# Two pieces of VectorE work given to other engines in the first pairs of a fused attention and expert kernel

## The chip, the cores and the metric

The kernel runs on one core of one Trainium2 chip. The core has five engines with a queue each, and each queue runs its instructions in order: TensorE (PE, with its weight loads PEld), VectorE (DVE), ScalarE (ACT), GpSimd (POOL) and SyncE (SP, which here only issues transfers). The metric is the device time of one execution in microseconds (us), the median of several runs.

## The reference, cut to what matters

Attention by random features feeds a gated expert layer, and that feeds a second expert layer. There are 8 batches of 576 tokens, 8 heads of 64, a model width of 512 and a hidden width of 1024.

```python
proj = q @ w_phi                                  # also for k, per head
proj = proj - max(abs(proj), axis=-1)
q_p, k_p = concat(exp(proj), exp(-proj))          # 256 features
num = q_p @ (k_p.T @ v);  den = q_p @ sum(k_p) + 1e-6
x = num / den                                     # 8 heads side by side: width 512
xk = mu_k * x + (1 - mu_k) * x_prev               # x_prev: the token before
xr = mu_r * x + (1 - mu_r) * x_prev               # these two are "the mixes"
y = sigmoid(xr @ w_r) * (relu(xk @ w_k) ** 2 @ w_v)
h = relu(y @ w_in);  out = (h * sigmoid(conv3(h)) @ w_out)
```

## The kernel before, in words

The attention works on pairs of heads, 32 of them (4 for each batch), numbered from 0. For each pair, TensorE projects the keys (`pk`, two tiles of 512 columns) two pairs ahead and the queries (`pq`) one pair ahead, and the last 64 tokens apart (`p`). VectorE takes the largest magnitude of each (`mx`) and subtracts it (`t`, `centre`, lines 328 to 332). TensorE turns the queries (`pt`, `pr`), ScalarE takes the exponentials (`kp`, `kr`, `qf`), TensorE sums keys and values (`pkv`, copied to `kvf` by ScalarE) and multiplies (`pn`). `results` (lines 411 to 429) scales: two small additions and a reciprocal give `rd`, two instructions of VectorE scale the first 512 tokens of the two heads into `xn` (tokens by width), and a third scales the last 64 tokens (line 428). TensorE turns `xn` into `xT` by way of `px` and `pr`, and ScalarE copies it (`column`, `column_end`).

When the four pairs of a batch are there, the first expert layer takes the batch in two halves of 288 tokens (`moe(u)`, u from 0 to 15). The mixes of a half are made in `mix(u, j)`, lines 483 to 502, j = 0 for xk and 1 for xr, in four parts of 128 rows. For u = 0, ScalarE writes `mu * x` to `mh` and VectorE adds `(1 - mu) * x_prev` in one instruction (line 491). For later halves a temporary `xf` is made likewise, then split into a coarse part (`mh`, ScalarE) and the rest (`ml`, VectorE). The products are `psk` (w_k), `psr` (w_r) and `psv` (w_v); `kf`, `kh`, `sg` and `x` are what ScalarE and VectorE make of them.

The weights come in 64 bit floats and are converted on the way, in 20 steps, numbered here from 0: steps 0 to 7 are w_k, 8 and 9 half of w_r, 10 to 13 half of w_v, 14 and 15 the rest of w_r, 16 to 19 the rest of w_v. A step (lines 204 to 219) is a load `raw` by SP (512 KB, three buffers), `h<-raw` on ScalarE, `h<-h` on GpSimd, `h<-h` and twice `h<-raw,h` on VectorE, and a transfer by SP into its place (`wkl<-h`, `wrh<-h`, `wvl<-h`). SP's queue takes these transfers in a fixed order: the write of step n stands ahead of the load of step n + 3.

TensorE's order is written out by hand. The orders of the other engines come from the framework's list scheduler, which runs a model of the engines while the program is built: a changed instruction can move its neighbours. `behind` (line 69) pins an instruction behind the last one given to its engine. The temporaries of the expert layers come from a pool of four buffers (`tmps`). `ORDER` (line 24) says in which order the buffers of four tile groups come up in the last stage, where it serves to choose offsets.

Of the kernel before, what the change touches and what calls it, by code (L numbers as in the profile page):

```python
# [8 lines left out]
F32 = mybir.dt.float32  # L9
F32R = mybir.dt.float32r  # L10
U32 = mybir.dt.uint32
AF = mybir.ActivationFunctionType
ALU = mybir.AluOpType
AX = mybir.AxisListType

P = 128
B, H, S, D = 8, 8, 576, 64
# [3 lines left out]
FC = DFF // P  # L21
TMPS = 4
XT = 6
ORDER = {"kh": (0, 3, 2, 1), "kl": (0, 3, 2, 1), "mh": (0, 1), "ml": (0, 1)}
PSM = 3


# [2 lines left out]
MS, SLOW, SR = 4, 8, {4: 6, 5: 6, 6: 7, 7: 9}  # L30
# [5 lines left out]
HS = S // 2  # L36
# [9 lines left out]
def fused_kernel(ctx: ExitStack, tc: tile.TileContext, qk, va, wphi, ones2, mu, wk, wv, wr, win, wout, cw, out):  # L46
# [29 lines left out]
    T, V, A, G = Noted(nc.tensor), Noted(nc.vector), Noted(nc.scalar), Noted(nc.gpsimd)  # L76
# [3 lines left out]
    tmps = ctx.enter_context(tc.tile_pool(name="tmps", bufs=TMPS))  # L80
# [3 lines left out]
    def f(x):  # L84
        return x.bitcast(F32)
# [29 lines left out]
    mu1 = const.tile([P, 2, KC], F32, name="mu1")  # L115
# [13 lines left out]
    def place(tag, name, c, dtype=F32R):  # L129

        return tagged(tag, name, dtype)[:, 7:7 + (KC if tag[0] == "m" else 2) * HS].rearrange("p (a n) -> p a n", a=c)

    def place2(tag, name, i, n):

        o = -(BASE[tag] + 16 * i) % 64
        return tagged(tag, name)[:, o:o + n]
# [53 lines left out]
    with ExitStack() as p1:  # L190
# [66 lines left out]
        for h in range(2):  # L257
            for w in ((wr, wrh, wrl), (wv, wvh, wvl)):
                n = w[1].shape[1] // 2
# [9 lines left out]
        xT = {}  # L269
# [141 lines left out]
        def results(Pi, qf):  # L411

            kv = kvs.pop(Pi)
            pn = [psa.tile([P, 512], F32, tag="at", name="pn")[:, :n * V1].rearrange("p (a n) -> p a n", n=V1) for n in (5, 4)]
            prods = [(0, 0, j, c) for j in range(4) for c in range(2)] + [(0, None, 4, c) for c in range(2)]
            prods += [(1, 1, j, c) for j in range(4) for c in range(2)]
            for b_, h, j, c in prods:
                for r in range(2):
                    h_, o = (r, 512) if h is None else (h, j * P + 64 * r)
                    T.matmul(pn[b_][64 * r:64 * r + 64, j], qf[h_][:, c, o:o + 64], kv[:, c, h_], start=(j == 0 and c == 0), stop=(j == 4 - b_ and c == 1))  # L420
            rd = pool.tile([P, 9], F32, tag="rd4", bufs=2, name="rd")
            V.tensor_scalar(rd[:, :5], pn[0][:, :, D], 1e-6, None, ALU.add)
            V.tensor_scalar(rd[:, 5:], pn[1][:, :, D], 1e-6, None, ALU.add)
            V.reciprocal(rd, rd)
            xn = xns[Pi] = pool.tile([P, 5, P], F32, tag="xn", bufs=1, name="xn")
            for h in range(2):
                V.tensor_tensor(xn[:, :4, D * h:D * h + D], pn[h][:, :4, :D], rd[:, 5 * h:5 * h + 4].unsqueeze(2).to_broadcast([P, 4, D]), ALU.mult)
            V.tensor_scalar(xn[:, 4].rearrange("p (a n) -> p a n", a=2), pn[0][:, 4:5, :D].to_broadcast([P, 2, D]), rd[:, 4:5], None, ALU.mult)
            del ts[Pi]

        xns = {}
# [5 lines left out]
        def block(Pi):  # L437
# [26 lines left out]
            if Pi >= 0:  # L464
                results(Pi, qf)
# [17 lines left out]
        def mix(u, j):  # L483

            b, hf = divmod(u, 2)
            o = hf * HS
            hi = place("mh", f"mh{j}", KC, F32R if u else F32)
            if u == 0:
                for c in range(KC):
                    (A.behind if j else A.do)("activation", hi[:, c], xT[b, c][:, 1 + o:1 + o + HS], AF.Copy, scale=mu0[:, j, c:c + 1])  # L490
                    (V.behind if j else V.do)("scalar_tensor_tensor", hi[:, c], xT[b, c][:, o:o + HS], mu1[:, j, c:c + 1], hi[:, c], ALU.mult, ALU.add)
                return hi, hi
            lo = place("ml", f"ml{j}", KC)
            for c0 in range(0, KC, 2):
                xf = tmps.tile([P, 2, HS], F32, tag="tmp", name="xf")
                for c in range(c0, c0 + 2):
                    late = (u, j) == (1, 1)
                    (A.behind if late else A.do)("activation", xf[:, c - c0], xT[b, c][:, 1 + o:1 + o + HS], AF.Copy, scale=mu0[:, j, c:c + 1])
                    (V.behind if late else V.do)("scalar_tensor_tensor", xf[:, c - c0], xT[b, c][:, o:o + HS], mu1[:, j, c:c + 1], xf[:, c - c0], ALU.mult, ALU.add)
                A.copy(hi[:, c0:c0 + 2], xf)  # L500
                V.tensor_tensor(lo[:, c0:c0 + 2], xf, f(hi[:, c0:c0 + 2]), ALU.subtract)
            return hi, lo
# [3 lines left out]
        def mix_next(u, j):  # L506
            if (u, j) in mixed:
                return True
            if u >= 2 * B or any((u // 2, c) not in xT for c in range(KC)):
                return False  # L510
            mixed[u, j] = mix(u, j)
            if j and u % 2:
                done[0] = u // 2 + 1
            return True
# [145 lines left out]
    with ExitStack() as p2:  # L660
# [17 lines left out]
        def load_x2(i):  # L678
            lo, hi = U * i, U * i + U
            xs_ = []  # L680
            for c in range(0, KC, 2):
                if i % 2:
                    xh, xl = [place2(t, m_, ORDER[t][c // 2], 2 * U).rearrange("p (a n) -> p a n", a=2) for t, m_ in (("mh", "xh"), ("ml", "xl"))]
                else:
# [12 lines left out]
        def up(i, fc, xs_):  # L697
# [34 lines left out]
            if fc >= 4 and end:  # L732
                if not fc % 2:
                    last[:] = [place2(t_, m_, ORDER[t_][fc // 2 - 2], U + 64 + n) for t_, m_ in (("mh", "gh"), ("ml", "gl"))]
                o = fc % 2 * (U + 64)
                gh, gl = [x[:, o:o + n] for x in last]
            elif fc < 4:
                gh, gl = [place2(t_, m_, ORDER[t_][fc], n) for t_, m_ in (("kh", "gh"), ("kl", "gl"))]
            else:
# [101 lines left out]
```

## Time and profile before

| | us |
|---|---|
| median of 3 runs | 1203.96 |
| lowest and highest run | 1203.6, 1205.41 |
| the profiled execution | 1204.29 |
| its span, first to last instruction | 1202.3 |
| PE busy | 1187.5 (99%) |
| DVE busy | 751.4 (62%) |
| ACT busy | 687.7 (57%) |
| POOL busy | 142.9 (12%) |

Times are counted from the first instruction, and 1.99 us of the profiled execution lie outside the span. The granted TensorE clock is 1.00 in every stretch. The shares hide the beginning: in the first 64 us VectorE is nearly always busy and TensorE is not, and after about 123 us TensorE hardly ever stops.

### The profile page before, as it was taken

Reading aid. Unit: us, or ns where it says so; the run is one execution under the profiler, and the core shown is the slowest. Engines: PE = TensorE matmul, PEld = TensorE weight load, DVE = VectorE, ACT = ScalarE, POOL = GpSimd, SP = SyncE. Lnnn points to the kernel's source line nnn. Section 1 sums busy time; section 2 is a strip of 40 time slices with the busy share of each in tenths; the row PEclk is TensorE's granted clock in tenths of the full one; section 3 lists DMA queues with packets and bytes.
Section 4 is the critical chain, followed back from the end, with each engine's and each line's share of the span. In section 5 each row is a group of like instructions: output and inputs, shape, how many; then the busy total and the mean of one; then the engine's idle time right before and its main releaser. Section 6 shows DMA issues by size and latency. Waiting matters only on the chain.

```text
span 1202.3 us, 28950 instructions
## 1 busy us (share of the span) xinstructions
PE 1187.5 (99%) x11842; PEld 1097.7 (91%) x11842; DVE 751.4 (62%) x1525; ACT 687.7 (57%) x1604; POOL 142.9 (12%) x353
## 2 busy tenths in 40 slices
PE   7999999999999999999999999999999999999998
PEld 7887999999999999999999999998888888888888
DVE  7988776576675765767646534426557556645744
ACT  5765865576565664665645534426546555655653
POOL 2122101111111110211000000001101111111200
PEclk9999999999999999999999999999999999999999
DMA  6666222234232322332110004050221121022021
GB/s 231 222 194 230 62 76 59 87 94 125 88 94 77 107 96 87 95 98 88 50 52 23 12 21 161 20 195 1 71 71 29 42 71 40 31 71 59 12 71 36
DMA packets 57252, 100.76 MB, mean 84 GB/s; under 512 B 8864, under 2 KB 38304, under 8 KB 57120
## 3 DMA queue, kind: packets, MB, share of 16 engines
q1 hardware_dynamic: 40848, 61.59, 15.4%
q0 software_dynamic: 6768, 27.69, 7.5%
q10 hardware_dynamic: 9504, 9.64, 2.9%
q8 instruction: 93, 1.52, 0.5%
q14 instruction: 39, 0.32, 0.1%
HBM read 66.38 MB, written 27.27 MB: 78 GB/s over the span
## 4 chain that ended last, share of the span: by engine, by line
PE 92%; DVE 3%; issue 2%; ACT 2%; DMA 1%; POOL 0%; POOLq 0%; ACTq 0%; DVEq 0%
PE psk L61 16%; PE pso L61 16%; PE psh L61 16%; PE psv L61 16%; PE psr L61 8%; PE pkv L61 5%; PE pn L61 4%; PE pk L61 2%; PE pq L61 2%; PE pt L61 2%; DVE mx L61 1%; PE px L61 1%; DVE h L61 1%; PE p L61 1%; DVE t L61 1%
## 5 line engine op out<-in xcount | busy, mean ns | idle before, releaser
L61 DVE SCALAR_TENSOR_TENSOR ct<-h,cw,ct 128x513 f32<-128x513 f32 (+1 forms) x144 | 108.2, 751 | 84.5 <-ACT ct L61 83.2
L61 PE MATMUL psv<-kh,wvl 128*128 128x288 f32 x544 | 156.6, 306 | 0.6 <-DMA wvl<-h 0.4
L61 PE MATMUL psk<-mh,wkl 128*128 128x288 f32 x544 | 155.4, 304 | 0.0
L61 PE MATMUL psv<-kl,wvh 128*128 128x288 f32 x480 | 141.2, 295 | 0.0
L61 PE MATMUL psk<-ml,wkh 128*128 128x288 f32 x480 | 140.4, 293 | 0.0
L61 PE MATMUL psv<-kh,wvh 128*128 128x288 f32 x480 | 140.1, 292 | 0.0
L61 PE MATMUL psk<-mh,wkh 128*128 128x288 f32 x480 | 139.5, 291 | 0.0
L61 PE MATMUL pso<-gl,woh 128*128 128x512 f32 (+2 forms) x320 | 115.7, 367 | 0.0
L61 PE MATMUL pso<-gh,woh 128*128 128x512 f32 (+2 forms) x320 | 115.6, 367 | 0.0
L61 ACT ACTIVATE kf<-psk 128x288 f32<-128x288 f32 x128 | 52.1, 407 | 107.7 <-PE psk L61 106.9
L61 PE MATMUL psh<-xh,wih 128*128 128x512 f32 x288 | 111.4, 389 | 0.0
L61 PE MATMUL psh<-xl,wih 128*128 128x512 f32 x288 | 111.2, 389 | 0.0
L61 PE MATMUL psh<-xh,wil 128*128 128x512 f32 x288 | 108.0, 389 | 0.0
L61 PEld LDWEIGHTS psv<-kh,wvl 128*128 128x128 f32 x544 | 102.1, 188 | 5.0 <-DMA wvl<-h 0.8
L61 PEld LDWEIGHTS psk<-mh,wkl 128*128 128x128 f32 x544 | 101.9, 188 | 3.4
L61 PE MATMUL psr<-mh,wrh 128*128 128x288 f32 x512 | 103.1, 299 | 0.0
L61 PE MATMUL pso<-gh,wol 128*128 128x512 f32 (+2 forms) x320 | 102.2, 367 | 0.0
L61 PEld LDWEIGHTS psv<-kh,wvh 128*128 128x128 f32 x480 | 90.5, 189 | 0.0
L61 PEld LDWEIGHTS psv<-kl,wvh 128*128 128x128 f32 x480 | 89.7, 187 | 0.8
L61 PEld LDWEIGHTS psk<-ml,wkh 128*128 128x128 f32 x480 | 89.8, 187 | 0.1
L61 PEld LDWEIGHTS psk<-mh,wkh 128*128 128x128 f32 x480 | 89.8, 187 | 0.0
L61 ACT ACTIVATE kp<-t 128x512 f32<-128x512 f32 x128 | 70.1, 617 | 33.0 <-PE pkv L61 30.6
(101 smaller groups left out, 2609.2 us busy)
## 6 DMA issues: line engine op xcount, KB each, us to landing
rqk<-qk POOLq DMA_DIRECT2D x29, 576.0 KB, 4.6
va<-va POOLq DMA_DIRECT2D x30, 325.0 KB, 4.6
x2s<-x SPq DMA_DIRECT2D x30, 288.0 KB, 2.3
raw<-wk SPq DMA_DIRECT2D x8, 512.0 KB, 5.2
raw<-wv SPq DMA_DIRECT2D x8, 512.0 KB, 4.4
raw<-win SPq DMA_DIRECT2D x16, 256.0 KB, 2.9
raw<-wout SPq DMA_DIRECT2D x16, 256.0 KB, 2.9
wkl<-h SPq DMA_DIRECT2D x8, 256.0 KB, 2.5
```

What stands on the lines that cost most here:

```text
L61: x = op(*a, **k)
```

## The change

Two pieces of VectorE's work go to other engines. In the mixes of the first half (u = 0, eight instructions of VectorE), GpSimd now makes `(1 - mu) * x_prev` into a temporary `x0` and adds it to `mh`: two instructions in place of one. For pairs 0 to 7, ScalarE scales the last 64 tokens (`MS + SLOW // 2` is 8). `ORDER` is changed in one entry.

```diff
-ORDER = {"kh": (0, 3, 2, 1), "kl": (0, 3, 2, 1), "mh": (0, 1), "ml": (0, 1)}
+ORDER = {"kh": (0, 3, 2, 1), "kl": (0, 3, 1, 2), "mh": (0, 1), "ml": (0, 1)}
...
-            V.tensor_scalar(xn[:, 4].rearrange("p (a n) -> p a n", a=2), pn[0][:, 4:5, :D].to_broadcast([P, 2, D]), rd[:, 4:5], None, ALU.mult)
+            last4 = xn[:, 4].rearrange("p (a n) -> p a n", a=2), pn[0][:, 4:5, :D].to_broadcast([P, 2, D])
+            if Pi < MS + SLOW // 2:
+                A.activation(*last4, AF.Copy, scale=rd[:, 4:5])
+            else:
+                V.tensor_scalar(*last4, rd[:, 4:5], None, ALU.mult)
...
-                    (V.behind if j else V.do)("scalar_tensor_tensor", hi[:, c], xT[b, c][:, o:o + HS], mu1[:, j, c:c + 1], hi[:, c], ALU.mult, ALU.add)
+                    x0 = tmps.tile([P, HS], F32, tag="tmp", name="x0")
+                    (G.behind if j else G.do)("tensor_scalar", x0, xT[b, c][:, o:o + HS], mu1[:, j, c:c + 1], 0.0, ALU.mult, ALU.add)
+                    G.tensor_tensor(hi[:, c], hi[:, c], x0, ALU.add)
```

The orders of TensorE and SP stay the same, row for row. Those of VectorE, ScalarE and GpSimd change until about pair 7 and are the same behind it. Three places of VectorE's queue follow.

The first is behind the scaling of pair 0 (`xn`), the difference of the two orders; `mx<-p_471` and `t<-p_471` centre the last 64 tokens of a pair, and the `h` rows are weight step 1:

```order
 L61 TENSOR_TENSOR xn<-pn,rd 128x4x64 x2
-L61 TENSOR_SCALAR xn<-pn,rd 128x128
-L61 TENSOR_SCALAR h<-h 128x512
 L61 TENSOR_REDUCE mx<-p_471 128x2
-L61 SCALAR_TENSOR_TENSOR h<-raw,h 128x512
 L61 TENSOR_TENSOR t<-p_471,mx 128x256
-L61 SCALAR_TENSOR_TENSOR h<-raw,h 128x512
```

The scaling of the last tokens is gone from the queue, and weight step 1 has moved behind the centring of `pk`, into that of `pq`. Pair 2 (steps 4 and 5) is changed in the same way.

The second place is behind the scaling of pair 5, before the change; the `h` rows are the end of weight step 11 (the first three instructions) and step 12, and `xf` the four parts of a mix of the second half:

```order
L61 TENSOR_SCALAR xn<-pn,rd 128x128
L61 TENSOR_SCALAR h<-h 128x512
L61 SCALAR_TENSOR_TENSOR h<-raw,h 128x512 x2
L61 SCALAR_TENSOR_TENSOR xf<-xT,mu_79,xf 128x288
L61 TENSOR_SCALAR h<-h 128x512
L61 SCALAR_TENSOR_TENSOR xf<-xT,mu_79,xf 128x288
L61 SCALAR_TENSOR_TENSOR h<-raw,h 128x512
L61 SCALAR_TENSOR_TENSOR xf<-xT,mu_79,xf 128x288 x2
L61 SCALAR_TENSOR_TENSOR h<-raw,h 128x512
```

The same place in the changed order, where the first `h<-h` and the two `h<-raw,h` are step 11:

```order
L61 TENSOR_TENSOR xn<-pn,rd 128x4x64 x2
L61 SCALAR_TENSOR_TENSOR xf<-xT,mu_79,xf 128x288
L61 TENSOR_SCALAR h<-h 128x512
L61 SCALAR_TENSOR_TENSOR xf<-xT,mu_79,xf 128x288
L61 SCALAR_TENSOR_TENSOR h<-raw,h 128x512
L61 SCALAR_TENSOR_TENSOR xf<-xT,mu_79,xf 128x288 x2
L61 SCALAR_TENSOR_TENSOR h<-raw,h 128x512
L61 TENSOR_SCALAR h<-h 128x512
```

Step 11 was done ahead of all four parts of the mix and is now done behind them; step 12 has moved back by as much.

The third place is the end of the conversion, around the scaling of pair 6, before the change; the rows `h<-raw,h` at the top end steps 16 and 17, the two `h<-h` begin steps 18 and 19:

```order
L61 SCALAR_TENSOR_TENSOR h<-raw,h 128x512 x2
L61 TENSOR_SCALAR rd<-pn 128x5
L61 SCALAR_TENSOR_TENSOR h<-raw,h 128x512
L61 TENSOR_SCALAR rd<-pn 128x4
L61 RECIPROCAL rd<-rd 128x9
L61 TENSOR_TENSOR xn<-pn,rd 128x4x64 x2
L61 TENSOR_SCALAR xn<-pn,rd 128x128
L61 TENSOR_SCALAR h<-h 128x512
L61 SCALAR_TENSOR_TENSOR h<-raw,h 128x512 x2
L61 SCALAR_TENSOR_TENSOR x_1578<-sg,psv 128x288
L61 TENSOR_SCALAR h<-h 128x512
L61 SCALAR_TENSOR_TENSOR h<-raw,h 128x512 x2
```

The same place in the changed order, where the first four `h<-raw,h` belong to steps 16, 17, 16 and 17, in this order:

```order
L61 TENSOR_SCALAR rd<-pn 128x5
L61 SCALAR_TENSOR_TENSOR h<-raw,h 128x512 x2
L61 TENSOR_SCALAR rd<-pn 128x4
L61 SCALAR_TENSOR_TENSOR h<-raw,h 128x512 x2
L61 RECIPROCAL rd<-rd 128x9
L61 TENSOR_TENSOR xn<-pn,rd 128x4x64 x2
L61 SCALAR_TENSOR_TENSOR x_1594<-sg,psv 128x288
L61 TENSOR_SCALAR h<-h 128x512
L61 SCALAR_TENSOR_TENSOR h<-raw,h 128x512 x2
L61 TENSOR_SCALAR h<-h 128x512
L61 SCALAR_TENSOR_TENSOR xf<-xT,mu_79,xf 128x288 x2
L61 SCALAR_TENSOR_TENSOR h<-raw,h 128x512 x2
```

Step 16 ends one `rd` and two or three `h` rows later, and between the first instruction of step 19 and its other two stand two parts of a mix. On ScalarE the new scaling stands behind the exponentials `qf` or `kr` of its block, and the `h<-raw` that stood ahead of those now stands behind it.

## Rows read from the trace of the kernel before

**Rows 1.** Busy time by stretch (--windows): length, then each engine, granted clock, DMA.

```profile
12.00:64.00 52.00, 47.98 (x1043) 43.24 (x1039) 49.43 (x107) 39.00 (x103) 11.58 (x19) 1.00 0.63 200
...
123.00:1202.30 1079.30, 1074.34 (x10178) 1000.88 (x10176) 648.63 (x1308) 606.65 (x1404) 116.31 (x299) 1.00 0.22 69
```

**Rows 2.** What TensorE waited for from 12 to 123 us: total, times, longest.

```profile
PE pk L61 <- DVE xn L61: 2.1, 3, 0.9
PE pt L61 <- DVE t L61: 1.9, 3, 1.1
```

**Rows 3.** VectorE in order of time, pair 1: start, us, instruction, idle before.

```profile
25.66 0.34 DVE L61 TENSOR_SCALAR xn<-pn,rd 128x128 f32<-128x128 f32 x1
...
27.52 1.06 DVE L61 SCALAR_TENSOR_TENSOR h<-raw,h 128x512 uint32<-128x512 uint32 x1
28.51 1.27 DVE L61 TENSOR_REDUCE mx<-pk 128x4 f32<-128x512 f32 x2
...
30.90 0.50 DVE L61 SCALAR_TENSOR_TENSOR mh<-xT,mu,mh 128x288 f32<-128x288 f32 x1
31.33 0.41 DVE L61 TENSOR_SCALAR h<-h 128x512 uint32<-128x512 uint32 x1
...
36.44 0.34 DVE L61 TENSOR_SCALAR xn<-pn,rd 128x128 f32<-128x128 f32 x1
36.70 0.42 DVE L61 TENSOR_REDUCE mx<-p 128x2 f32<-128x256 f32 x1
```

**Rows 4.** TensorE in order of time: `pk` in pairs 1 to 3.

```profile
36.67 1.25 PE L61 MATMUL pk<-wp,rqk 64*128 64x128 f32 x16 [0.53 <-DVE xn L61]
...
46.02 1.28 PE L61 MATMUL pk<-wp,rqk 64*128 64x128 f32 x16
...
56.65 1.25 PE L61 MATMUL pk<-wp,rqk 64*128 64x128 f32 x16 [0.92 <-DVE xn L61]
```

**Rows 5.** ScalarE: `kr` (--tile: durations min/median/max, ns), and `qf` of pair 2 in order.

```profile
L61 ACT ACTIVATE kr<-t x24: 290/302/312, 6.4 to 110.1; 128x128 f32<-128x128 f32 x12, 64x128 f32<-64x128 f32 x12
...
45.04 2.02 ACT L61 ACTIVATE qf<-pt 128x512 f32<-128x512 f32 x4
```

**Rows 6.** GpSimd in order of time, two weight steps of different length.

```profile
27.43 0.61 POOL L61 TENSOR_SCALAR h<-h 128x512 f32<-128x512 f32 x1 [2.39 <-ACT h L61]
...
95.38 1.59 POOL L61 TENSOR_SCALAR h<-h 128x512 f32<-128x512 f32 x1 [3.54 <-ACT h L61]
```

**Rows 7.** ScalarE in order of time, weight steps 13 and 15.

```profile
90.48 0.66 ACT L61 ACTIVATE h<-raw 128x512 f32<-128x512 f32 x1 [2.95 <-DMA raw<-wv]
91.05 1.37 ACT L61 ACTIVATE xf<-xT,mu 128x288 f32<-128x288 f32 x3
...
98.80 0.67 ACT L61 ACTIVATE h<-raw 128x512 f32<-128x512 f32 x1 [3.21 <-DMA raw<-wr]
```

**Rows 8.** VectorE in order of time, weight steps 11 and 12.

```profile
87.70 1.43 DVE L61 SCALAR_TENSOR_TENSOR h<-raw,h 128x512 uint32<-128x512 uint32 x2
...
93.53 0.68 DVE L61 SCALAR_TENSOR_TENSOR h<-raw,h 128x512 uint32<-128x512 uint32 x1
```

**Rows 9.** SP's queue in order of time: loads 15 and 19.

```profile
94.80 0.54 SPq L207 DMA_DIRECT2D raw<-wr  x1
...
110.01 0.53 SPq L207 DMA_DIRECT2D raw<-wv  x1
```

**Rows 10.** TensorE in order of time, 92 to 123 us, where it waited.

```profile
92.76 4.16 PE L61 MATMUL psv<-kh,wvl 128*128 128x288 f32 x16 [0.27 <-ACT kf L61]
...
100.00 1.16 PE L61 MATMUL pk<-wp,rqk 64*128 64x128 f32 x14 [0.80 <-ACT xT L61]
...
121.08 2.22 PE L61 MATMUL psv<-kh,wvl 128*128 128x288 f32 x8 [0.38 <-DMA wvl<-h]
```

**Rows 11.** The chain that ended last, in order of time: weight step 19.

```profile
110.01 5.36 DMA raw<-wv
...
118.76 2.27 DMA wvl<-h
```

## The prediction

> **What bounds the kernel now.** I read the windows first. From 123 us to the end TensorE is busy 1074.34 of 1079.30 us; from 12 to 64 us it is busy 47.98 of 52.00, and VectorE 49.43 [rows 1]. The change works only in pairs 0 to 7, so it can save only what TensorE idles ahead of 123 us. The waits say for whom: 2.1 us for VectorE's scaling `xn`, 1.9 for its centring `t` [rows 2]. The third view, order in time, shows that these waits lie in every second pair: TensorE works through from `pk` at 36.67 to `pk` at 46.02, so a pair cannot take less than 9.35 us, while the next takes 10.63 [rows 4]. Behind 64 us TensorE waits three times: 0.27, 0.80 for ScalarE's `xT`, and 0.38 for the write of weight step 19 [rows 10]. This last wait decides my forecast: the chain behind it is the conversion of the weights.
>
> **What it removes in the first stretch.** The scaling of the last tokens holds VectorE for 0.26 us (36.44 to 36.70), the addition of a mix for 0.43 (30.90 to 31.33) [rows 3]. Pairs 0 to 3 are up to the first expert products, so 4 x 0.26 + 3 x 0.43, 2.3 us of VectorE's time, go where it is short. Not all of it is gained, since in the new order weight step 1 no longer fills the time in which VectorE waits for `pk`. Pair by pair:
> - `pk` behind pair 0 waits for the last `xn`; it loses 0.26 of that wait.
> - In pair 1 VectorE's stretch from `xn` to `xn` was 36.44 - 25.66 = 10.78 [rows 3]. It loses 0.69. Now it waits for `pk`, which takes TensorE 1.25 us [rows 4] from about 25.8, until 27.0, while the centring of `p` (two instructions of 0.42 [rows 3], the second begun 0.33 behind the first) ends at 26.4. That is 0.6 of idling. The slow `h<-raw,h` at 27.52 is gone, 1.06 where 0.68 is usual [rows 3, 8]: 10.78 - 0.69 - 0.38 + 0.6 = 10.3. TensorE's `pk` starts some 0.5 us early in all.
> - Pair 2 fills TensorE already: nothing.
> - Pair 3 goes like pair 1. The wait of 0.92 at 56.65 [rows 4] shrinks by another 0.25, since of the two weight steps that stood early three instructions now stand just ahead of `xn`.
> I take a gain of 0.75 us; the ends are 2.9 (the sum of all waits of rows 2 behind the first `pt`, 2.1 + 1.9 - 1.1) and -0.5 (below).
>
> **What it adds.** ScalarE gets eight scalings of 128 x 128; `kr` of the same shape takes 0.30 [rows 5]. TensorE's `px` and `pr` now wait for it. It stands behind four `qf`. In pair 2 these ended at 45.04 + 2.02 = 47.06 [rows 5], where `px` stood 1.2 us behind `pk` at 46.02 [rows 4]; the `h<-raw` that stood ahead of them moves behind the scaling, so the 0.30 fits, with some 0.2 us to spare here and about 0.6 in the pairs that wait. If that cover were gone, each of four pairs would lose up to 0.3. GpSimd gets 16 instructions. Its `h<-h` of 512 columns takes 0.61 [rows 6]; 288 columns of the same kind are 0.35 to 0.4 us by that. The addition with two inputs is not in this trace: its ends are 0.35 (as the other) and 1.59, the slow row of this engine [rows 6]; I take 0.7, nearer to the usual 0.61. GpSimd is busy 11.58 of 52 us [rows 1], `psk` and `psr` use the mixes several us later, and its loads `rqk` and `va` wait for TensorE anyway: on the path this costs nothing. The temporaries `x0` are read at once, so `tmps` is not short.
>
> [...] At 27.43 GpSimd's `h<-h` ran [rows 6] while VectorE's `h<-raw,h`, which reads two tiles of SBUF, took 1.06 in place of 0.68 [rows 3, 8]. [...]
>
> **What it moves: the weights.** SP's order is unchanged: the load of step n + 3 goes out only behind the write of step n. So whatever makes a step late makes the third step after it late. Two places are moved.
>
> Step 11. VectorE ended it at 87.70 + 1.43 = 89.1 [rows 8]. In the new order its two `h<-raw,h` stand behind all four `xf` (second place shown above). ScalarE makes the second `xf` only behind `h<-raw` of step 13, for which it waited 2.95 us until 90.48 [rows 7]. So step 11 ends where step 12 ended, 93.53 + 0.68 = 94.2 [rows 8], less the 0.75 gained: its write goes out at 93.5. With 2.3 us for the transfer [rows 11] it lands at 95.8. TensorE needs it for the second half of the first `psv` block, which began at 92.76 and took 4.16 [rows 10]: at 94.8, less 0.75, 94.05. It stalls for 1.8 us, and is 1.1 late against before in place of 0.75 early.
>
> `pk` at 100.00. It waited 0.80 for `xT`, which stood on ScalarE behind `h<-raw` of step 15 [rows 7, 10]. Now it stands behind that of step 14, whose load takes the time of load 15: 94.80 to 98.80 [rows 7, 9], less 0.75. TensorE, 1.1 late, is there behind it: that wait is gone, and TensorE is 0.3 late.
>
> Step 16. The centring of `pk` in pair 6 follows a weight step on VectorE, 15 before and 14 now, and so starts some 0.8 early. But behind it the queue now holds step 15 whole and half of 17 ahead of the end of 16: three `h<-raw,h` at 0.6 to 0.7 (two took 1.43 [rows 8]), one `h<-h` (0.41 [rows 3]) and two short `rd` more than before, together 2.4. Step 16 ends 1.6 late, and so goes out load 19: 110.01 + 1.6 = 111.6 [rows 9].
>
> Step 19. Load 19 took 5.36 [rows 11]; the loads before it 4.0 (load 15). The loads of queries and keys now go out earlier and collide less with it: I take 4.8, landing at 116.4. Before, 5.66 us passed from 110.01 + 5.36 to the end of the write at 118.76 + 2.27 [rows 11]. Now two `xf` stand in between, which wait on ScalarE behind a weight copy (0.6), two `sg` (0.35 each) and themselves; beside GpSimd's own part that is 1.3 us more. The write lands at 123.35, and TensorE goes on at 123.4 in place of 121.08 [rows 10].
>
> **The sum.** At that place TensorE is 2.3 late: 0.75 gained, 1.8 lost to step 11, 0.80 given back, and there 2.4 of waiting in place of 0.38. From there the queues are the same as before and TensorE is full: the 2.3 us stay. The profiled execution took 1204.29, so 1206.6; the median is 0.33 below it, so 1206.3, 0.19% above before. Its own range comes from load 19, 4.0 to 5.4 us (-0.9, +0.5), and the gain ahead, 0.3 to 1.2 (+0.45, -0.45): 1205.0 to 1207.3.
>
> **The rivals.**
> 1. The weights keep up and the first gain stays. One mechanism: if load 13 lands 2 us earlier than its `h<-raw` at 90.48, the `xf` no longer hold step 11, and the ring of three runs ahead. For it: step 12's copy did not wait. Against: 2.95 us of waiting for load 13, and a faster start does not make it land sooner relative to step 10. Then 0.75 to 1.9 us (with 0.80 and 0.38) are gained, 1203.2 to 1202.0: I take 1202.8, not slower.
> 2. Only step 11 stalls: step 19 lands in time if load 19 takes 3 us or less, or if TensorE has been held up elsewhere by as much. Then TensorE is 0.3 late and the wait of 0.38 gone: as before, 1203.9. Against: loads 15 and 19 took 4.0 and 5.4.
> 3. GpSimd and VectorE get in each other's way. Eight new GpSimd instructions in the first stretch at the 0.38 of the row at 27.52 are 3.0 us, more than the 2.3 removed; the gain of 0.75 is lost, and the rest of the sum remains: 1207.1. For it: that row, and the 1.59 [rows 6]. [...]
> 4. ScalarE's scaling comes late for `px`, by up to 0.3 in four pairs: the gain turns into -0.5 and the end is 1207.6. Against: in three of four pairs 0.6 us are free.
>
> **Chances.** Forecast 0.52, rival 1 0.14, rival 2 0.13, rival 3 0.14, rival 4 0.07. A measurement of this kernel tells about 0.2%, 2.4 us, from no change: slower begins at 1206.4. Of the forecast somewhat under half lies above that, of rivals 3 and 4 nearly all; of rival 1 a quarter could be faster by as much. So slower 0.40, within 0.55, faster 0.05. The range leaves a tenth out at each side: 1202.8 to 1208.2.
>
> **What would show it.** Right: `pk` behind pair 1 starts near 36.2 and `psk` 0.75 us early; in the conversion the write of step 11 goes out near 93.5 and TensorE waits about 1.8 us for it in the first `psv` block; `pk` in pair 6 waits no more for `xT`; load 19 goes out near 111.5, and TensorE waits some 2.4 us for the last write. Wrong: no wait for a write of `wvl` at 94 us (rival 1), a wait there alone (rival 2), `h<-raw,h` of 1 us and more beside GpSimd's mixes (rival 3), `px` waiting for ScalarE (rival 4). The forecast falls if TensorE passes the last `psv` block ahead of 121 us.

## The result, and the profile after

| | us |
|---|---|
| median of 6 runs | 1210.32 |
| lowest and highest run | 1209.33, 1212.33 |
| the kernel before, 6 runs beside it | 1203.85 |
| ratio, 95% interval | 1.0056 [1.0045, 1.0066] |
| the profiled execution, its span | 1210.16, 1208.4 |

The change costs 6.5 us. The forecast, 1206.3, had the sign; the range (up to 1208.2) did not hold the time.

The same two stretches as in [rows 1] (the second ends with the longer span), with the same columns, of the changed kernel:

```profile
12.00:64.00 52.00, 47.07 (x1017) 42.58 (x1015) 47.50 (x98) 39.39 (x106) 15.59 (x26) 1.00 0.63 199
123.00:1208.40 1085.40, 1079.07 (x10187) 1004.80 (x10185) 650.51 (x1311) 607.92 (x1406) 116.49 (x301) 1.00 0.22 69
```

VectorE did lose work in the first stretch, 49.43 to 47.50 us, but TensorE was not busier for it: 47.98 to 47.07. And behind 123 us TensorE's busy time grew by 4.7 us, from 1074.34 to 1079.07. Nine more matmuls there (10187 against 10178), left over because TensorE comes late, are some 2.3 of that, as an estimate from a `psv` block of 16 in 4.16 us [rows 10]; the rest is the same matmuls taking longer. What TensorE waited for from 12 to 130 us (total, times, longest):

```profile
PE psv L61 <- DMA wvl<-h: 3.8, 5, 1.6
PE pk L61 <- DVE xn L61: 3.7, 4, 1.4
PE pt L61 <- DVE t L61: 1.3, 1, 1.3
PE psv L61 <- ACT kf L61: 0.8, 1, 0.8
```

Against [rows 2], the wait for `t` shrank from 1.9 to 1.3, the one for `xn` grew from 2.1 to 3.7, and the one for writes of `wvl` from one of 0.38 [rows 10] to five of 3.8 together. TensorE in order of time, the places of [rows 4] and [rows 10]:

```profile
36.54 1.25 PE L61 MATMUL pk<-wp,rqk 64*128 64x128 f32 x16 [1.20 <-DVE xn L61]
46.52 1.25 PE L61 MATMUL pk<-wp,rqk 64*128 64x128 f32 x16 [0.59 <-DVE xn L61]
57.09 1.33 PE L61 MATMUL pk<-wp,rqk 64*128 64x128 f32 x16 [1.42 <-DVE xn L61]
...
93.69 2.21 PE L61 MATMUL psv<-kh,wvl 128*128 128x288 f32 x8 [0.76 <-ACT kf L61]
97.51 2.22 PE L61 MATMUL psv<-kh,wvl 128*128 128x288 f32 x8 [1.61 <-DMA wvl<-h]
101.62 1.06 PE L61 MATMUL pk<-wp,rqk 64*128 64x128 f32 x16
...
124.84 2.21 PE L61 MATMUL psv<-kh,wvl 128*128 128x288 f32 x8 [1.35 <-DMA wvl<-h]
```

The loss has two parts. The first is made by 131 us. Its cause stands in ScalarE's queue; pair 0, then pair 5, in order of time:

```profile
22.93 0.35 ACT L61 COPY kvf<-pkv 128x260 f32<-128x260 f32 x1
23.19 0.51 ACT L61 ACTIVATE kr<-t 128x128 f32<-128x128 f32 x2
24.25 2.06 ACT L61 ACTIVATE qf<-pt 128x512 f32<-128x512 f32 x4 [0.55 <-PE pt L61]
26.18 0.39 ACT L61 ACTIVATE xn<-pn,rd 128x128 f32<-128x128 f32 x1
26.42 0.70 ACT L61 ACTIVATE h<-raw 128x512 f32<-128x512 f32 x1
...
87.45 0.37 ACT L61 ACTIVATE xn<-pn,rd 128x128 f32<-128x128 f32 x1 [1.62 <-DVE xn L61]
87.72 1.23 ACT L61 ACTIVATE h<-raw 128x512 f32<-128x512 f32 x2
88.85 0.38 ACT L61 ACTIVATE kf<-psk 128x288 f32<-128x288 f32 x1
```

The same two `h<-raw` (steps 1 and 11) in the kernel before:

```profile
23.19 0.68 ACT L61 ACTIVATE h<-raw 128x512 f32<-128x512 f32 x1
...
84.27 0.67 ACT L61 ACTIVATE h<-raw 128x512 f32<-128x512 f32 x1
```

They came 3.2 and 3.5 us earlier. The scaling waits for the end of its pair, and the weight step's `h<-raw` is pinned behind it (line 211: `A.behind`, behind the last operation given to ScalarE, which the scaling now is). So the whole step is late. On VectorE steps 1 and 2 now come one behind the other, just ahead of the scaling of pair 1, on TensorE's path (the first row is the end of step 1 and the middle of step 2, the last row the end of step 2):

```profile
33.20 1.29 DVE L61 SCALAR_TENSOR_TENSOR h<-raw,h 128x512 uint32<-128x512 uint32 x2
34.40 0.16 DVE L61 TENSOR_SCALAR rd<-pn 128x5 f32<-128x5 f32 x1
34.52 0.69 DVE L61 SCALAR_TENSOR_TENSOR h<-raw,h 128x512 uint32<-128x512 uint32 x1
```

The second part is lost evenly from 131 to 806 us, with no new wait (from 137 us on TensorE waits 1.3 us in all, in both kernels). The matmuls of `psk` in one stretch (first number behind the comma: busy us, count), before and then after:

```profile
450.00:600.00 150.00, 37.94 (x288) 37.62 (x288) 9.79 (x24) 1.00 0.28 84
```

```profile
450.00:600.00 150.00, 38.27 (x288) 37.96 (x288) 9.78 (x24) 1.00 0.28 86
```

The difference is 0.33 us for 288, so some 1.5 for the 1344 of the 14 halves from 181 us on; most of the rest is in `psv`. From start to start a `psk` matmul takes 131.1 ns, and before 130.0 (means over 137 to 800 us). The clock is 1.00 in both.

### The profile page after: what moved, and what is told of

Same layout as the page of the kernel before. It is cut to its first block, busy times and chain, and to the rows that moved or that the text cites. A ratio compares the mean times of both kernels' runs of the same rounds, so it can differ in the third digit from the quotient of the medians.

```text
span 1208.4 us, 28971 instructions
## 1 busy us (share of the span) xinstructions
PE 1189.0 (98%) x11842; PEld 1098.3 (91%) x11842; DVE 747.3 (62%) x1509; ACT 689.8 (57%) x1612; POOL 151.7 (13%) x369
## 4 chain that ended last, share of the span: by engine, by line
PE 91%; DVE 3%; issue 2%; ACT 1%; DMA 1%; POOL 1%; SPq 0%; POOLq 0%; DVEq 0%; ACTq 0%
PE pso L61 16%; PE psh L61 16%; PE psk L61 16%; PE psv L61 16%; PE psr L61 8%; PE pkv L61 5%; PE pn L61 5%; PE pk L61 2%; PE pq L61 2%; PE pt L61 2%; DVE h L61 1%; PE px L61 1%; DVE mx L61 1%; PE p L61 1%; PE pr L61 1%
```

## The experiments

All times are against the kernel before, on the same chip as the experiment. The starting theory (A): the order of weight steps 11 and 19 on VectorE costs the time, as forecast, and the buffers the rest. Its rival (B): GpSimd and VectorE collide.

**Each half alone.** In the first, the mixes are VectorE's again:

```diff
-                    x0 = tmps.tile([P, HS], F32, tag="tmp", name="x0")
-                    (G.behind if j else G.do)("tensor_scalar", x0, xT[b, c][:, o:o + HS], mu1[:, j, c:c + 1], 0.0, ALU.mult, ALU.add)
-                    G.tensor_tensor(hi[:, c], hi[:, c], x0, ALU.add)
+                    (V.behind if j else V.do)("scalar_tensor_tensor", hi[:, c], xT[b, c][:, o:o + HS], mu1[:, j, c:c + 1], hi[:, c], ALU.mult, ALU.add)
```

> Only half of the change: ScalarE scales the last 64 tokens' results of pairs 0 to 7, VectorE keeps its part of the mixes. In this program VectorE's weight steps 11 and 19 stand behind the xf of the second half's mixes, as in the changed kernel, and the kl buffers rotate as in the changed kernel. Theory A (the order of the weight steps, then the buffers): nearly the whole loss is here, 1208.5 to 1211 us, with TensorE's matmuls of step 11's columns waiting about 1.5 us for the DMA of wvl and those of step 19's some 1.3 us, and psk matmuls after 137 us 131.1 ns apart instead of 130.0. Theory B (GpSimd and VectorE collide): this half costs nothing, 1203 to 1205 us.

Measured: 1212.15, ratio 1.0071 [1.0056, 1.0086], above the range that A gave. TensorE's waits:

```profile
PE psv L61 <- DMA wvl<-h: 3.8, 5, 1.6
PE pk L61 <- DVE xn L61: 3.5, 2, 1.9
```

Part of this time is the clock. In the profiled execution TensorE waits 1.95 us for `xn` until 57.37, and from about 59.0 to 62.4 the granted clock is 0.50; there the 16 matmuls of `pq` take 2.08 us, and 1.16 at 48.09 in the same trace. Without a wait TensorE loses 1.5 us there: against the kernel before it is 0.72 late ahead of that stretch and 2.25 behind it. Of the four executions the one with a mean clock of 1.000 took 1211.37. What lets the clock fall is open: a wait of 1.99 at 102.53 in the kernel with a tile of its own, below, brought no such stretch (granted clock 1.00 from 76 to 130 us).

```profile
59.00:62.00 3.00, 3.00 (x29) 2.44 (x29) 3.00 (x7) 1.43 (x4) 0.12 (x1) 0.50 0.58 225
```

In the second, the scaling is VectorE's again (and `ORDER` as before, since the buffers rotate as before):

```diff
-            if Pi < MS + SLOW // 2:
+            if False:
```

> Only the other half: GpSimd does VectorE's part of the first half's mixes, VectorE scales the last 64 tokens as before. Steps 11 and 19 stand on VectorE where they stand in the kernel before, and kl rotates as before. Theory A: no loss, 1203 to 1204.5 us, matmuls of psk 130.0 ns apart after 137 us. Theory B: the loss is here, 1207 us or more, with VectorE's weight steps at 1.4 us instead of 0.4 us beside GpSimd's additions several times.

Measured: 1202.85, ratio 0.9992 [0.9983, 1.0002], just below A's range. TensorE's waits are those of the kernel before, those for VectorE shorter, and none for a weight:

```profile
PE pk L61 <- DVE xn L61: 1.9, 3, 0.7
PE pt L61 <- DVE t L61: 1.3, 1, 1.3
PE pk L61 <- ACT xT L61: 0.8, 1, 0.8
PE psv L61 <- ACT kf L61: 0.4, 1, 0.4
```

The whole loss is in the scaling; the mixes on GpSimd even bring 1.5 us by 131 us in the trace. B falls as the cause of the loss. The collision itself is there, and dearer than in [rows 3]: here are GpSimd's addition and, from the same trace, VectorE's `h<-h`, which takes 0.42 in most places.

```profile
39.66 0.69 POOL L61 TENSOR_TENSOR mh<-mh,x 128x288 f32<-128x288 f32 x1 [0.43 <-ACT mh L61]
```

```profile
39.70 0.94 DVE L61 TENSOR_SCALAR h<-h 128x512 uint32<-128x512 uint32 x1
```

It happens four times up to 75 us (`h<-h` 0.94 and 0.91, `h<-raw,h` 1.12 and 0.79), some 1.5 us of VectorE's time in all, less than was taken from it.

In the changed kernel it reaches TensorE. There `h<-h` of pair 2 takes 1.42, a full 1.00 more:

```profile
40.11 1.42 DVE L61 TENSOR_SCALAR h<-h 128x512 uint32<-128x512 uint32 x1
```

```profile
40.53 0.71 POOL L61 TENSOR_TENSOR mh<-mh,x 128x288 f32<-128x288 f32 x1
```

`xn` follows at 45.62, and TensorE waits the 0.59 at 46.52 shown above. With the scaling alone, where VectorE makes the mixes, nothing is lost in that pair (last table, `pk` 36.67 and 46.02).

**The order of steps 11 and 19 restored** on VectorE, in the changed kernel:

```diff
+PIN = {0: 11, 1: 19}
...
+            ends.append(V.last)
             SY.dma_start(f(ls[:, o_]), h)
...
+                    if u == 1 and j in PIN:
+                        tc.add_manual_dep(V.last, ends[PIN[j]].name, mybir.DependencyInfo(mybir.DependencyClass.NoSync, mybir.DependencyReason.DATA), reason="order")
```

> The changed kernel, with the xf of the second half's first mix pinned behind step 11 on VectorE and those of the second mix behind step 19, as they stand before the change; nothing else moves, and the kl buffers stay as in the changed kernel. Theory A: TensorE's waits for wvl at step 11 and step 19 shrink by about 1.3 and 1.1 us, so the start of the second half comes 2 to 3 us earlier; the slower matmuls after it (2.2 us in all) stay: 1206.8 to 1208.3 us. Theory B: 1209.5 to 1210.5 us, as changed.

Measured: 1210.92, ratio 1.0053 [1.0037, 1.0070]. A's forecast fails. Step 11's write goes out at 91.16 in place of 95.16 and its stall is gone, but TensorE then stops for later steps:

```profile
114.08 2.19 PE L62 MATMUL psr<-mh,wrh 128*128 128x288 f32 x8 [1.72 <-DMA wrh<-h]
118.15 4.13 PE L62 MATMUL psv<-kh,wvl 128*128 128x288 f32 x16 [1.88 <-DMA wvl<-h]
123.20 2.19 PE L62 MATMUL psv<-kh,wvl 128*128 128x288 f32 x8 [0.92 <-DMA wvl<-h]
```

The order on VectorE makes the stall at step 11, but is not the root of the loss: the steps come to VectorE late. That led to ScalarE's queue above, and to theory C: the pin of `h<-raw` behind the scaling. Its rival D: the scaling's own 0.37 us on ScalarE and the hand-over between the engines.

**The pin taken away.** The scaling is issued past the object that remembers the last operation. The `kl` buffers then rotate as before, and `ORDER` with them; all else is kept:

```diff
-                A.activation(*last4, AF.Copy, scale=rd[:, 4:5])
+                nc.scalar.activation(*last4, AF.Copy, scale=rd[:, 4:5])
```

> The whole change, with one difference: the scaling on ScalarE is issued without being remembered as ScalarE's last operation, so the next weight step's Abs is no longer ordered behind it and keeps the place it had before the change; the kl buffers then rotate 0, 3, 2, 1 again. Theory C (the loss is the pin: Abs waits behind a scaling that waits for VectorE, the weight steps come late and the buffers rotate otherwise): 1201.5 to 1203.5 us, no wait of TensorE for wvl above 0.5 us, psk matmuls 130.0 ns apart. Rival D (the scaling's 0.37 us on ScalarE, and the hand-over from VectorE to ScalarE and back, cost the time wherever the Abs stands): 1207 to 1210 us.

Measured: 1203.55, ratio 1.0001 [0.9992, 1.0010]. ScalarE in pair 0: `h<-raw` is back at 23.09, and the scaling stands where it stood in the changed kernel.

```profile
22.83 0.36 ACT L61 COPY kvf<-pkv 128x260 f32<-128x260 f32 x1
23.09 0.69 ACT L61 ACTIVATE h<-raw 128x512 f32<-128x512 f32 x1
...
26.08 0.39 ACT L430 ACTIVATE xn<-pn,rd 128x128 f32<-128x128 f32 x1
```

No wait for `wvl` is left. C held, D fell, but the time is at the upper end of what C expected: a gain of 1.6 us at 64 us is given back: 0.5 us ahead of the first `psv`, and 1.5 at one new wait, since a step's `h<-raw` now stands between the two halves of `qf` (ScalarE, at 100.83) and waits 1.00 for its load:

```profile
PE pkv L61 <- ACT qf L61: 1.5, 1, 1.5
```

**The wait without the work.** To the kernel before, one column copied by ScalarE where the scaling would stand:

```diff
             V.tensor_scalar(xn[:, 4].rearrange("p (a n) -> p a n", a=2), pn[0][:, 4:5, :D].to_broadcast([P, 2, D]), rd[:, 4:5], None, ALU.mult)
+            if Pi < MS + SLOW // 2:
+                A.copy(pool.tile([P, 1], F32, tag="one", bufs=2, name="one"), rd[:, 4:5])
```

> The kernel before, with nothing moved; at the place of the scaling of pairs 0 to 7 ScalarE copies one column of rd to a spare tile, remembered as its last operation, so that the next Abs stands behind it. It adds the wait and next to no work. Theory C: most of the loss of the change comes back, 1208 to 1212 us, with kl rotating 0, 3, 1, 2. Rival D: 1203.5 to 1205 us.

Measured: 1211.54, ratio 1.0064 [1.0049, 1.0080]: 7.8 us for eight copies of 0.19. By 131 us 4.1 are lost, by 806 us another 2.3 in the slower matmuls, and 1.5 in the last stage. There `ORDER` doesn't fit the rotation 0, 3, 1, 2 that this copy causes; the changed kernel, with the same rotation and an `ORDER` that fits, loses nothing there. ScalarE in pair 0:

```profile
24.96 0.19 ACT L61 COPY one<-rd 128x1 f32<-128x1 f32 x1
25.05 0.66 ACT L61 ACTIVATE h<-raw 128x512 f32<-128x512 f32 x1
```

**A tile of its own** for the scaled last tokens, in the unpinned kernel:

```diff
-            xn = xns[Pi] = pool.tile([P, 5, P], F32, tag="xn", bufs=1, name="xn")
+            xn = xns[Pi] = pool.tile([P, 4, P], F32, tag="xn", bufs=1, name="xn")
+            x4s[Pi] = pool.tile([P, P], F32, tag="x4", bufs=2, name="x4")
...
-            T.transpose(px[:, :P], xn[:, 4], ident)
+            T.transpose(px[:, :P], x4, ident)
```

> As the kernel with the scaling unpinned, and ScalarE's result goes to a tile of its own, so that the scaling waits for the reciprocal alone, not for VectorE's first xn, and VectorE's xn no longer waits for ScalarE. Theory C: the scaling starts some 0.5 us earlier in each pair and VectorE's gap of 0.3 to 0.5 us between reciprocal and xn goes; each of pairs 1 and 3 may start pk 0.1 to 0.3 us earlier: 0 to 1 us less than with the shared tile. If the shared tile is not on the path: equal within 0.2%.

Measured: 1203.32, ratio 0.9998 [0.9989, 1.0007]; not to be told from the shared tile in time. The wait through the shared tile was real (the row below names `kr` as what ended it, but it goes when the tile is no longer shared). In the unpinned kernel, pair 5, VectorE:

```profile
84.11 0.22 DVE L61 RECIPROCAL rd<-rd 128x9 f32<-128x9 f32 x1
84.81 0.75 DVE L61 TENSOR_TENSOR xn<-pn,rd 128x256 f32<-128x256 f32 x2 [0.48 <-ACT kr L61]
```

and with the tile of its own:

```profile
84.04 0.22 DVE L61 RECIPROCAL rd<-rd 128x9 f32<-128x9 f32 x1
84.29 0.76 DVE L61 TENSOR_TENSOR xn<-pn,rd 128x256 f32<-128x256 f32 x2
```

**The slower matmuls: the rotation of `kl`.** In the changed kernel the four `kl` buffers come up in the order 0, 3, 1, 2, before it 0, 3, 2, 1 (the entry in `ORDER` follows that). The tiles that `psk` reads and writes lie at the same addresses in both. The kernel before, with this rotation alone, each buffer with a tag of its own:

```diff
+        if tag == "kl":
+            n = 3 if name == "taps" else turns[0] % 4
+            turns[0] += name != "taps"
+            bufs, tag = 1, f"kl{ROT[n]}"
...
+    ROT = (0, 3, 1, 2)
```

> The kernel before, in which only the rotation of the four kl buffers is that of the changed kernel (0, 3, 1, 2 instead of 0, 3, 2, 1; the three taps instructions stand earlier). Theory A2 (the gradual loss after 125 us comes from where the kl tiles lie): the stretch to 125 us as before, then 2.2 us lost evenly up to 800 us, psk matmuls 131.1 ns apart instead of 130.0: 1205.6 to 1206.5 us. Rival A3 (it comes from something else that differs: the tmp buffers, the PSUM banks of attention, or the state in which TensorE enters the second half): 1203.5 to 1204.3 us with 130.0 ns.

Measured: 1207.20, ratio 1.0028 [1.0017, 1.0038], above A2's range; the profiled execution, 1206.41, was one of the fastest, and its trace accounts for 2.1 us of the loss. A3's forecast fails. The `psk` row, as of the changed kernel:

```profile
450.00:600.00 150.00, 38.27 (x288) 37.96 (x288) 9.81 (x24) 1.00 0.28 84
```

Two more rotations, in the unpinned kernel and in the one below, by the same edit (`ROT` and the `kl` entry of `ORDER`):

> As the kernel with the scaling unpinned, with the four kl buffers made to rotate 0, 1, 2, 3 instead of 0, 3, 2, 1. Theory E (the pitch of the matmuls after 137 us is set by where the kl tiles of neighbouring steps lie): a pitch of psk of its own, between 129.5 and 131.5 ns, constant from half to half; each 0.1 ns of psk and psv is 0.3 us, so the time is 1201 to 1205 us. Rival (the pitch is decided by the state in which TensorE enters the second half): 130.0 ns as in the kernel that it is made from.

Measured: 1205.47, ratio 1.0014 [1.0005, 1.0023], against 1203.55 of the kernel it is made from, and above E's range.

> As the kernel with the scaling in pairs 0 to 2 only, with the kl buffers rotating 0, 2, 1, 3. Theory E (where neighbouring kl tiles lie sets the pitch): a constant pitch per kind of matmul, other than 0, 3, 2, 1 has; 0, 3, 1, 2 and 0, 1, 2, 3 gave 131.1 ns for psk and 0.6 to 2.2 us lost by 800 us, so 1202 to 1205 us. If the order with odd distances (0, 3, 2, 1) is not special: as the kernel it is made from, within 0.5 us.

Measured: 1205.45, ratio 1.0014 [1.0005, 1.0023], against 1202.52, and again above E's range. The edit costs something by itself: it moves a few instructions of the other engines (`taps` and the last weight steps), and at 131 us the three kernels with it are 0.2, 0.6 and 0.9 us behind those that they are made from.

What the stretch from the `psk` block at 131.6 us to the first `psh` at 806 us takes longer than in the kernel before (differences of the blocks' starts in the traces), and the mean from start to start of the `psk` matmuls:

| kernel | `kl` rotation | lost from 131.6 to 806, us | `psk`, ns |
|---|---|---|---|
| before | 0, 3, 2, 1 | 0 | 130.0 |
| mixes alone; unpinned; three pairs | 0, 3, 2, 1 | 0.0, -0.1, 0.0 | 130.0 |
| changed; before with the rotation | 0, 3, 1, 2 | 2.3, 2.1 | 131.1 |
| unpinned with the rotation | 0, 1, 2, 3 | 1.4 | 131.1 |
| three pairs with the rotation | 0, 2, 1, 3 | 1.5 | 131.1 |

Theory E holds in part: the pitch goes with the rotation, but the three other rotations share one pitch where E expected one for each, and the rotation is not all of it. In two kernels with 0, 3, 1, 2 one block of the 14 had 130.0 (at 713 us in the kernel before with the rotation, at 719 with the steps pinned). No run has the separate tags with 0, 3, 2, 1, so for the last two rows of the table the edit's own part is open; for 0, 3, 1, 2 the changed kernel has the same pitch without the tags.

Why stays open. `psk` doesn't read `kl`; only `psv` does, which runs ahead of it. But VectorE writes `kl` while `psk` runs, here inside the block that began at 131.63 in the kernel before, and no run tried whether that matters:

```profile
138.18 0.76 DVE L61 TENSOR_TENSOR kl<-kf,kh 128x576 fp32r<-128x576 f32 x1 [1.67 <-ACT kh L61]
```

**A version that beats both.** The unpinned kernel, with ScalarE's scaling in the first three pairs only:

```diff
-            if Pi < MS + SLOW // 2:
+            if Pi < 3:
```

> As the kernel with the scaling unpinned, but ScalarE scales in pairs 0 to 2 only; from pair 3 on VectorE does it as before. GpSimd does the first half's mixes. Theory C: the gain of the first 64 us stays (pk of pair 3 some 1.5 us earlier than in the kernel before), and ScalarE's order near 100 us is that of the kernel with the mixes alone, so TensorE's 1.5 us wait for qf ahead of pkv goes: 1.5 to 2.2 us less than the kernel before at 131 us, 1201.5 to 1202.8 us. Rival: each gain of the first stretch is given back at a later wait, as in the unpinned kernel: 1203 to 1204 us.

Measured: 1202.52, ratio 0.9989 [0.9980, 0.9998], 1.2 us faster than the kernel before, which was 6.5 faster than the changed one. From the mixes alone (1202.85, ratio 0.9992) it can't be told: at 131 us it is 1.45 early and they are 1.54. So the gain is the mixes' on GpSimd, and ScalarE's scaling brings nothing that lasts. The wait for `qf` is gone:

```profile
PE pk L61 <- DVE xn L61: 1.8, 3, 0.8
PE pt L61 <- DVE t L61: 1.3, 1, 1.3
PE psv L61 <- ACT kf L61: 0.9, 1, 0.9
PE pk L61 <- ACT xT L61: 0.9, 1, 0.9
```

How much later (+) or earlier (-) TensorE's blocks start than in the kernel before, us:

| block, start before | changed | scaling alone | mixes alone | steps pinned | unpinned | three pairs | wait alone |
|---|---|---|---|---|---|---|---|
| `pk` 36.67 | -0.13 | +0.20 | -0.54 | -0.31 | -0.99 | -0.96 | +0.62 |
| `pk` 46.02 | +0.51 | +0.19 | -0.45 | +0.33 | -0.87 | -0.84 | +0.63 |
| `psk` 64.18 | +0.52 | +2.25 | -1.12 | +0.27 | -1.60 | -1.56 | +1.00 |
| `psv` 92.76 | +0.92 | +2.50 | -1.04 | +1.01 | -1.11 | -1.01 | +1.59 |
| `pt` 97.19 | +2.81 | +4.38 | -1.04 | +1.01 | -1.11 | -1.01 | +2.44 |
| `pkv` 102.07 | +1.43 | +3.00 | -1.03 | -0.37 | +0.45 | -0.93 | +2.63 |
| `psk` 131.63 | +3.75 | +5.33 | -1.54 | +5.60 | -0.39 | -1.45 | +4.13 |

From `psk` 64.18 on, the column of the scaling alone holds the 1.5 us of the lower clock; without them it ends at some +3.8, as the changed kernel.

## Why the prediction was right and wrong

Of the 4.0 us between the forecast and the measurement 1.5 are there by 131 us and 2.3 come behind it; two steps failed.

- **The gain of the first stretch: the step that failed first.** Forecast 0.75 us early at `psk`, measured 0.52 late. `pk` of pair 1 is 0.13 early (forecast 0.5), pair 2, booked at nothing, gets a wait of 0.59, and the wait of 0.92 in pair 3 grows to 1.42 where it was to shrink. The forecast saw that "the `h<-raw` that stood ahead of them moves behind the scaling", and booked it as room for ScalarE; it didn't ask what waits for the moved `h<-raw`. That step was 3.2 us late, and its three VectorE instructions landed between `pk`'s centring and `xn`. Without the pin the same two moves bring 1.60 at `psk`, more than forecast: the time taken from VectorE was there to be gained.
- **Step 11.** Stall forecast 1.8, measured 1.61; the write at 93.5, measured 95.16, 1.3 of the 1.7 being the missing gain. The mechanism held: with the old order on VectorE this stall went. But it was not what the time hung on, since TensorE then waited longer for later steps; without the pin neither order nor stall was there.
- **The wait for `xT`** at 100.00 went, as forecast. **Load 19** went out at 113.55 (forecast 111.6). At the end of the conversion TensorE was 3.75 late in place of 2.3: the sum's 1.27 too much gain, and 0.2 from the other terms.
- **"From there the 2.3 us stay"** failed second: the queues are the same behind it, but another 2.3 us went to slower matmuls. The forecast held that TensorE, when it never waits, takes the same time; the change of `kl`'s rotation, visible in the `ORDER` entry, was read as a matter of offsets only.
- **The prices.** Scaling 0.37 to 0.39 (forecast 0.30), `x0` 0.50 (0.35 to 0.4), addition 0.69 (0.7). None of them decided.
- **Rivals.** 1 and 2 fell, five waits for `wvl`. 3: collisions took place, but the mixes alone lose nothing; in the changed kernel the one at 40.11 is behind the wait of 0.59 in pair 2, so this rival has a part in the missing gain. The rows at 39.66 and 39.70 show it for an instruction that the forecast did not count, `h<-h` with one input: 0.94 there, and 0.42 in most places for the 512 columns, where `h<-raw,h`, with two inputs, took 0.68. What holds it up is not shown. 4: `px` never waited for ScalarE; the scaling came late for what stood behind it, not for its reader.

## What to carry to other kernels

Moved to another engine, an operation was here above all a wait in that engine's queue: list what is pinned or queued behind it and follow that to its reader; its own length mattered least (eight of 0.37 us, which cost nothing without the pin, against 6.5 with it). Two cheap runs tell work from wait: the wait without the work, and the work without the pin. And where a stretch becomes slower evenly without a new wait, compare the pitch of equal matmuls (here 131.1 ns against 130.0) and the rotation of the buffers before looking for a stall.

## What the runs showed of the hardware that was not expected

- Matmuls of 288 columns on tiles at unchanged addresses took 130.0 or 131.1 ns from start to start, and which of the two went with the rotation of four other buffers, in all blocks from 181 us on but the two named above. The first `psk` block with split weights, at 131.6 us in the kernel before, had 131.1 behind its first matmul in all of these kernels but the unpinned one. What sets the pitch of a block is open.
- VectorE's `h<-h`, one input from SBUF, took 0.91 to 0.94 us in place of 0.42 beside GpSimd's addition of 0.69, and 1.42 in the changed kernel.
- While VectorE and ScalarE wrote different parts of one tile, in pair 5 of the unpinned kernel, VectorE's `xn` waited 0.48 us and ScalarE's 0.58; with a tile each VectorE's wait was gone.
- With the scaling alone the granted clock of TensorE stood at 0.50 from about 59.0 to 62.4 us, behind a wait of 1.95, and 1.5 us were lost without a wait.
